# Two more token blocks of batch 0 by the seven-product form, with the work around them re-ordered, in an attention and squared-ReLU kernel

## The chip, the core and the metric

The kernel runs on one core of a Trainium2 chip. The metric is the device time of one execution in microseconds (us); the figure for the kernel before is the median of six runs. A core has a matrix engine (PE, its weight loads are listed as PEld), a vector engine (DVE), an activation engine (ACT), a general engine (POOL) and a sync engine (SP). Each of them works through its own instructions in order and waits on semaphores for the others. DMAs are issued by SP, ACT and POOL.

## What is computed

First a two-way cross attention between 512 tokens and 32 state rows for each of 8 batches and 8 heads of width 64, then a feed-forward layer on all 4352 rows:

```python
scores = scale * x @ state^T ; a = softmax(scores) ; xread = a @ state
scores2 = scale * state @ x^T ; a2 = softmax(scores2) ; sread = a2 @ x
X = concat([xread, sread], rows)      # (B*(512+32), 512)
h = X @ w_in                          # 512 -> 2048
r = maximum(h, 0)
g = s * (r * r) + b
out = g @ w_out                       # 2048 -> 512
```

`s` and `b` are single numbers, so they are applied after the last product: `out = s * ((r*r) @ w_out) + b * colsum(w_out)`. Inputs and outputs are float32; the products run in float16 with float32 accumulation.

## The kernel before

**Stages.** One loop runs over the batches s = 0 to 7, and within a batch over 16 feature blocks f of 128 columns of the hidden layer. For the token rows `xread @ w_in` is not formed as such: `state @ w_in` (tile M) is made once a batch, and `h` of block f is M times the softmax shares (`mm1_x`, two matmuls of 512 columns, a PSUM bank of pool psH with two buffers). `mm1_close` (L388) lets ACT take the ReLU into a tile r (three buffers, a pair of blocks each) and lets DVE square the pair into a tile g (L402). While the hidden layer of batch s is made, PE also does the output product of batch s-1, cut into single matmuls ("items") which are handed out between the blocks. Attention work of the next batch (M, T, E, D, V) is placed at given blocks by `pieces` (L782); "ahead" there means before the hidden block.

**The output product, plain.** For batch 0, `mm2_part` (L458) multiplies 16 blocks of g (weights 128x128) with 512 columns of w_out into one bank for each of the four token blocks of 128 rows: `units` (L680). `evac` (L442) scales, adds the bias and writes a tile `osb`, and POOL issues its DMA of 256 KB.

**The output product, seven products.** For batches 1 to 7, and for the 256 state rows ("sr"), `fast_items` (L506) computes the 2x2 block product of (two halves of the tokens) x (two halves of the hidden features) with (two halves of the features) x (two halves of the output columns) by seven block products P1 to P7 instead of eight. Each is 8 matmuls of 256 columns for each 128 tokens. It needs differences of w_out quarters (`weight_sums`, tiles wd0 to wd3, once) and sums of token halves of g (`token_sum`, tiles s1 to s4, eight DVE instructions a batch). Three PSUM banks are used, each by more than one product in turn, without being cleared:

- A: P1, read into qa (L585); then P2 is added to it, and the sum is written out (`put`, L559);
- B: P6, read into u2 (L588); then P7 is added, read into u3 (L593); then P4 is added and written out;
- C: P5 is written out with u3; then P3 is added and written out with u2.

So a product that is added to a bank can't start before DVE has read what the bank held. `put` writes a tile `osb` (pool opool, three buffers, shared with `evac`), which POOL sends out; a fourth tile waits until the DMA of the first has landed. The order of the products is the list in L626 to L632; for the last batch the tail has its own order and its own outputs (`put_last`, L569, DMA on SP).

**What sets the order.** PE, SP and POOL run in the order of the program text (L691). DVE and ACT are ordered by a scheduler, except where `tc.issue_after(...)` pins an instruction behind a named one; `G["last"]` names the latest square, `G["relu"]` the latest ReLU. POOL's queue holds the input loads (`load_x`) and nearly all outputs.

**Names used below.** "f = 9" is feature block 9 of batch 1 unless said otherwise. NST is the number of batches whose state is transposed by PE (`att_stT`); for the others one DMA transpose, `stT_dma`, issued by SP in batch 2, makes the tile stT_all. `mm1_sr` makes the hidden layer of the state rows (h_sr) at the end. The tail loop from L901 hands out the last batch's items with `go(rest, n)` after each h_sr block.

Of the kernel before, what the change touches and what calls it, by code (L numbers as in the profile page):

```python
# [14 lines left out]
def kernel(  # L15
# [10 lines left out]
    nc = tc.nc  # L26
# [15 lines left out]
    FC = 512  # L42
    NFC = DF // FC
    NPE = 2
    NST = 5
    NDT = 3
    NH = DM // 2
    TH = S // 2
# [339 lines left out]
    def mm1_close(key, hps, ntok, f):  # L388
        if f % 2 == 0:
            R2[key] = rpool.tile([P, 2, ntok], FP16, name=f"r_{key}_{f}", tag="r")  # L390
        r16 = R2[key]
        if key == 0 and f in (1, 5):
            nc.vector.tensor_scalar(r16[:, f % 2], hps, 0.0, None, ALU.max)
        else:
            nc.scalar.activation(r16[:, f % 2], hps, AF.Relu)  # L395
            G["relu"] = nc.cur_bb.bb.instructions[-1]
        if f % 4 == 0:
            G4[key, f // 4] = gpool.tile([P, 4, ntok], FP16, name=f"g_{key}_{f}", tag="g")
        gt = G4[key, f // 4]
        G[key, f] = gt[:, f % 4]  # L400
        if f % 2 == 1:
            nc.vector.tensor_mul(gt[:, f % 4 - 1 : f % 4 + 1], r16, r16)  # L402
            G["last"] = nc.cur_bb.bb.instructions[-1]

# [37 lines left out]
    def evac(ops, key, rr, n0, n1, dmas):  # L442
        osb = opool.tile([P, n1 - n0], FP32, name=f"osb_{key}_{rr}_{n0}", tag="osb")
        nc.vector.scalar_tensor_tensor(osb, ops, s_bc, bias_bc[:, n0:n1], ALU.mult, ALU.add)
        for eng, p0, p1, dst in dmas:
            eng.dma_start(dst, osb[p0:p1])

# [29 lines left out]
    def weight_sums():  # L477
        out = [[], []]
        for j in range(2):
            b11, b12 = wo[j][:, :, 0:NH], wo[j][:, :, NH:DM]  # L480
            b21, b22 = wo[2 + j][:, :, 0:NH], wo[2 + j][:, :, NH:DM]
            t1, t2, t3, t4 = (wd[i][j] for i in range(4))
            out[0] += [(t1, b12, b11), (t2, b22, t1)]
            out[1] += [(t3, b22, b12), (t4, b21, t2)]
        out = out[0] + out[1][::2] + out[1][1::2]
        return [lambda o=o, a=a, c=c: nc.vector.tensor_sub(o, a, c) for o, a, c in out]

    SQ = {}

    def token_sum(b, i, j):  # L490
        n = (B * Ns if b == "sr" else S) // 2
        SQ[b, i, j] = spool.tile([P, 4, n], FP16, name=f"s{i}_{b}_{j}", tag="s")
        o = SQ[b, i, j]
        a11, a21 = G4[b, j][:, :, 0:n], G4[b, j][:, :, n:]
        if i == 3:
            nc.vector.tensor_sub(o, a11, a21)  # L496
            return
        a12, a22 = G4[b, 2 + j][:, :, 0:n], G4[b, 2 + j][:, :, n:]
        if i == 1:
            nc.vector.tensor_add(o, a21, a22)  # L500
        elif i == 2:
            nc.vector.tensor_sub(o, SQ[b, 1, j], a11)  # L502
        else:
            nc.vector.tensor_sub(o, a12, SQ[b, 2, j])  # L504

    def fast_items(b):  # L506
        acc = {}
        kept = {}
        th = (B * Ns if b == "sr" else S) // 2
        ni = th // P  # L510

        def spare(name):
# [4 lines left out]

        def lhs(p, k, i):
            c = P * i
            if p == 1:  # L520
                return G[b, k][:, c : c + P]
            if p == 2:
                return G[b, 8 + k][:, c : c + P]
            if p == 4:
                return G[b, 8 + k][:, th + c : th + c + P]
            si = {3: 4, 5: 1, 6: 2, 7: 3}[p]
            return SQ[b, si, k // 4][:, k % 4, c : c + P]

# [10 lines left out]
        def keep(name):  # L539
            if b == "sr":  # L540
                i = len(kept)
                kept[name] = own[0][:, i : i + 1]
            else:
                kept[name] = upool.tile([P, 2, NH], FP32, name=f"{name}_{b}", tag=name)
            return kept[name]

        def put(bank, add, j, n0):
            if b == "sr":
                ends.append(own[1][:, len(ends) : len(ends) + 1])
                osb = ends[-1]  # L550
            else:
                osb = opool.tile([P, ni, NH], FP32, name=f"osb_{b}_{j}_{n0}", tag="osb")
            if bank == "C" and b == last_b:
                for i in range(ni):
                    nc.vector.scalar_tensor_tensor(
                        osb[:, i], acc["C", i], s_bc, add[:, i], ALU.mult, ALU.add
                    )
            else:
                nc.vector.scalar_tensor_tensor(osb, acc[bank], s_bc, add, ALU.mult, ALU.add)  # L559
            if b == "sr":  # L560
                for i in range(4):
                    dst = out_BSn[4 * j + i, S:ST, n0 : n0 + NH]
                    eng = nc.sync if i % 2 else nc.scalar
                    eng.dma_start(dst, osb[Ns * i : Ns * i + Ns, 0])
                return
            dst = out_BSn[b, 0:S].rearrange("(q ci cj) n -> cj q ci n", ci=2, cj=2)
            nc.gpsimd.dma_start(dst[j][:, :, n0 : n0 + NH], osb)  # L567

        def put_last(i):  # L569
            if not ends:  # L570
                ends.append(spare("osb_last"))
            osb = ends[0][:, i]
            nc.vector.scalar_tensor_tensor(
                osb, acc["C", i], s_bc, kept["u2"][:, i], ALU.mult, ALU.add
            )
            dst = out_BSn[b, 0:S].rearrange("(q ci cj) n -> cj ci q n", ci=2, cj=2)
            nc.sync.dma_start(dst[0][i][:, NH:DM], osb)

        def blk(n0):
            return bias_bc[:, n0 : n0 + NH].unsqueeze(1).broadcast_to([P, ni, NH])  # L580
# [42 lines left out]
            elif k == 7 and i == ni - 1:  # L623
                done(p)

        order = [(1, 0, 8), (6, 0, 4), (2, 0, 3), (6, 4, 8), (2, 3, 8), (7, 0, 8)]  # L626
        order += [(5, 0, 8), (4, 0, 8), (3, 0, 8)]
        if b == last_b:
            order = [(1, 0, 8), (6, 0, 4), (2, 0, 4), (6, 4, 8), (2, 4, 5)]
            order += [(7, 0, 8), (2, 5, 8), (4, 0, 8)]  # L630
        if b == "sr":
            order = [(p, 0, 8) for p in (1, 6, 2, 7, 5, 4, 3)]  # L632
        out = [(p, k, i) for p, k0, k1 in order for k in range(k0, k1) for i in range(ni)]
        if b == last_b:
# [43 lines left out]


    units = []  # L680
    for i in range(NKF):
        units.append((0, 2 * (i // 8) + i % 2, i % 8 // 2))
    last_b = B - 1

    def unit(u):
# [5 lines left out]
    with tc.manual_schedule(engines={ET.PE, ET.SP, ET.Pool}):  # L691
# [90 lines left out]
        def pieces(s):  # L782
# [6 lines left out]
            def ahead(f, fn):  # L789
                out.setdefault((f, "ahead"), []).append(fn)  # L790
# [44 lines left out]
            if s == 2:  # L835
                at(1, lambda: att_srT_dma(0))
                at(8, lambda: att_V(1))
                at(12, lambda: att_srT_dma(1))
            ahead(10, lambda: att_V(s))
            if nb < B:  # L840
                ahead(10, lambda: att_M(nb, 2, "later"))
                ahead(10, lambda: att_M(nb, 3, "later"))
                at(10, lambda: A[nb]["M", 2]())
                at(12, lambda: A[nb]["M", 3]())
            if s == last_b:
                at(11, lambda: att_srT(s))
            else:
                at(12, lambda: att_srT_dma(s))
            if s == last_b:
# [7 lines left out]
        for s in range(1, B):  # L857
# [3 lines left out]
            first = coming[s][:16] if s in fast else []  # L861
            if s == 1:
                items = [[] for _ in range(NKF)]
                for f in [*range(5), *range(6, 14)]:
                    items[f] = [lambda u=todo.pop(0): unit(u)]
                items[14], items[15] = first[0:8], first[8:16]
            else:
                flat = coming[s - 1][16:] + first
                n = -(-len(flat) // NKF)
                items = [flat[n * f : n * f + n] for f in range(NKF)]  # L870
            for f in range(NKF):
                for fn in todo_s.get((f, "ahead"), []):
                    fn()
                if s > 1 and 4 <= f < 13:
                    for fn in items[f]:
                        fn()
                    items[f] = []
                mm1_x(s, f)
                if s > 1 and f in (4, 5):
                    with tc.issue_after(G["last"]):  # L880
                        token_sum(s - 1, 4, f - 4)
                if s in fast:
                    if f in ((7, 9) if s == 1 else (7, 11)):
                        with tc.issue_after(G["last"]):
                            token_sum(s, 3, f // 8)
                    if s == 1 and f in (13, 14):
                        with tc.issue_after(G["last"]):
                            token_sum(s, f - 12, 0)
                    if s > 1 and f in (11, 12):
                        token_sum(s, f - 10, 0)  # L890
                    if f == 15:
                        token_sum(s, 1, 1)
                        token_sum(s, 2, 1)
                for fn in todo_s.get(f, []):
                    fn()
                if s == 1 and 5 <= f < 13:
                    with tc.issue_after(G["last"]):
                        sums.pop(0)()
                for fn in items[f]:
                    fn()  # L900
        rest = coming[last_b][16:]  # L901
# [6 lines left out]
        for f in range(4, NKF):  # L908
# [4 lines left out]
                token_sum("sr", 3, f // 8)  # L913
            if f in (11, 12, 13):
                token_sum("sr", (1, 2, 4)[f - 11], 0)
            go(rest, 5)
            if f >= 12:
                go(rows, 2)
        go(rest, 4)
# [37 lines left out]
```

## Time and profile before

| | us |
|---|---|
| median of six runs | 210.3 |
| lowest and highest run | 209.38 and 212.44 |
| the profiled execution, its own time | 209.38 |
| its span, first to last instruction | 207.6 |

| part of the profiled execution | us |
|---|---|
| last matmul ends | 202.9 |
| last DVE instruction (osb_last) starts | 202.94 |
| last output DMA is issued by SP | 203.6 |
| end of the span | 207.6 |

The page gives the busy time of each engine, the span in slices, the DMA queues, the chain of work that ended last, and groups of instructions. Two things to know in reading it: matmuls are pipelined, so the duration of one (380 ns for 512 columns, 273 for 256) includes its way through the array, and the pace is read from the distance of starts; and an engine's idle time matters only where the chain passes through it. The lowest DVE load of a 10 us stretch is at the start; between 20 and 30 us it is busy for 5.30 us, between 40 and 50 us for 8.59.

### The profile page before, as it was taken

Reading aid. Unit: us, or ns where it says so; the run is one execution under the profiler, and the core shown is the slowest. Engines: PE = TensorE matmul, PEld = TensorE weight load, DVE = VectorE, ACT = ScalarE, POOL = GpSimd, SP = SyncE. Lnnn points to the kernel's source line nnn. Section 1 sums busy time; section 2 is a strip of 40 time slices with the busy share of each in tenths; the row PEclk is TensorE's granted clock in tenths of the full one; section 3 lists DMA queues with packets and bytes.
Section 4 is the critical chain, followed back from the end, with each engine's and each line's share of the span. In section 5 each row is a group of like instructions: output and inputs, shape, how many; then the busy total and the mean of one; then the engine's idle time right before and its main releaser. Section 6 shows DMA issues by size and latency. Waiting matters only on the chain.

```text
span 207.6 us, 4792 instructions
## 1 busy us (share of the span) xinstructions
PE 199.1 (96%) x1949; PEld 130.1 (63%) x1949; DVE 159.9 (77%) x275; ACT 126.7 (61%) x252; POOL 37.6 (18%) x64
## 2 busy tenths in 40 slices
PE   7988999999999999999999999999999999999990
PEld 2433343445766776677667766666767776878880
DVE  1587835979769985999589968996799687696861
ACT  3678865699476857775776577666766455433100
POOL 5970001411210231023102110211021102100210
PEclk9999999999999999999999999999999999999999
DMA  6999996999998694949743904340425012100342
GB/s 184 225 202 206 206 192 100 184 175 172 242 103 178 152 159 71 176 114 207 103 95 88 201 26 104 84 124 3 101 74 137 0 54 101 55 0 0 103 123 83
DMA packets 46491, 25.49 MB, mean 123 GB/s; under 512 B 31428, under 2 KB 44484, under 8 KB 46468
## 3 DMA queue, kind: packets, MB, share of 16 engines
q0 software_dynamic: 15536, 16.19, 40.4%
q1 hardware_dynamic: 30132, 8.62, 23.2%
q10 hardware_dynamic: 800, 0.36, 0.7%
q8 instruction: 15, 0.25, 0.5%
q14 instruction: 8, 0.07, 0.1%
HBM read 17.33 MB, written 8.91 MB: 126 GB/s over the span
## 4 chain that ended last, share of the span: by engine, by line
PE 90%; DVE 4%; ACT 3%; issue 0%
PE h L70 25%; PE oB L70 18%; PE oC L70 12%; PE oA L70 12%; PE o L70 7%; PE Mps L70 4%; PE warm_ps L70 3%; PE h_sr L70 2%; ACT r L395 2%; PE V L70 1%; PE oB_sr L70 1%; PE T L70 1%; DVE M L320 1%; PE oC_sr L70 1%; PE oA_sr L70 1%; DVE g L402 1%
## 5 line engine op out<-in xcount | busy, mean ns | idle before, releaser
L395 ACT ACTIVATE r<-h 128x512 f16<-128x512 f32 x126 | 74.4, 602 | 46.7 <-PE h L70 46.6
L70 PE MATMUL h<-a,M 128*128 128x512 f16 x256 | 74.3, 380 | 1.2 <-DVE M L320 0.6
L402 DVE TENSOR_TENSOR g<-r 128x1024 f16<-128x1024 f16 x64 | 43.5, 682 | 16.0 <-ACT r L395 15.4
L70 PEld LDWEIGHTS <-s 128*128 128x128 f16 x448 | 43.3, 98 | 17.1 <-DVE s L502 1.7
L70 PEld LDWEIGHTS <-g 128*128 128x128 f16 x400 | 37.7, 98 | 20.6 <-issue 5.2
L567 POOL DMA_DIRECT2D out_dram<-osb x27 | 18.2, 675 | 124.5 <-DVE osb L559 85.4
L70 PE MATMUL oB<-wd,s 128*128 128x256 f16 x224 | 32.6, 273 | 0.2 <-DVE u L588 0.2
L70 PEld LDWEIGHTS <-M 128*128 128x128 f16 x256 | 24.5, 98 | 12.9 <-issue 1.8
L70 PE MATMUL oA<-wo,g 128*128 128x256 f16 x224 | 31.7, 273 | 0.1
L297 ACT CAST M<-Mps 128x1024 f16<-128x1024 f32 x20 | 20.1, 1007 | 0.0
L70 PE MATMUL oC<-wd,s 128*128 128x256 f16 x112 | 16.5, 273 | 0.0
L70 PE MATMUL o<-wo,g 128*128 128x512 f16 x64 | 16.3, 381 | 0.0
L70 PE MATMUL oB<-wd,g 128*128 128x256 f16 x112 | 15.9, 273 | 0.0
L70 PE MATMUL oC<-wo,s 128*128 128x256 f16 x112 | 15.3, 273 | 0.0
L395 ACT ACTIVATE r_sr<-h_sr 128x256 f16<-128x256 f32 x16 | 6.1, 382 | 8.7 <-PE h_sr L70 8.7
L588 DVE SCALAR_TENSOR_TENSOR u<-oB,s_bc,qa 128x512 f32<-128x512 f32 x7 | 5.3, 751 | 6.1 <-PE oB L70 6.1
L234 ACT ACTIVATE E<-T 128x256 f16<-128x256 f32 x20 | 7.4, 384 | 4.0 <-PE T L70 4.0
L502 DVE TENSOR_TENSOR s<-s,g 128x1024 f16<-128x1024 f16 x14 | 9.6, 684 | 0.2
L70 PE MATMUL h_sr<-srdT,wi 128*128 128x256 f16 x64 | 9.6, 273 | 0.0
L504 DVE TENSOR_TENSOR s<-g,s 128x1024 f16<-128x1024 f16 x14 | 9.6, 684 | 0.0
L496 DVE TENSOR_TENSOR s<-g 128x1024 f16<-128x1024 f16 x14 | 9.6, 684 | 0.0
L500 DVE TENSOR_TENSOR s<-g,g 128x1024 f16<-128x1024 f16 x14 | 9.5, 682 | 0.0
(107 smaller groups left out, 206.0 us busy)
## 6 DMA issues: line engine op xcount, KB each, us to landing
out_dram<-osb POOLq DMA_DIRECT2D x31, 256.0 KB, 3.7
xn<-in_x_dram POOLq DMA_DIRECT2D x7, 512.0 KB, 8.7
wi<-in_moe_w_in_dram POOLq DMA_DIRECT2D x4, 512.0 KB, 9.0
wo<-in_moe_w_out_dram POOLq DMA_DIRECT2D x4, 512.0 KB, 15.9
xf<-in_x_dram SPq DMA_DIRECT2D x2, 512.0 KB, 4.8
out_dram<-osb_sr SPq DMA_DIRECT2D x8, 32.0 KB, 1.5
out_dram<-osb_sr ACTq DMA_DIRECT2D x8, 32.0 KB, 1.7
out_dram<-osb_last SPq DMA_DIRECT2D x2, 128.0 KB, 2.3
```

Source lines behind the costliest of these rows:

```text
L70: return nc.tensor.matmul(out, lhsT, rhs, start=start, stop=stop, tile_position=tp, is_transpose=is_transpose, skip_group_check=True,)
L234: nc.scalar.activation(a["E"][:, g, 256 * m : 256 * m + 256], Ts[m][:, g, :], AF.Exp, scale=scale, accum_out=a["rs"][:, NG * m + g : NG * ...
L297: nc.scalar.copy(dst, ps)
L320: nc.vector.tensor_copy(dst[:, 0], two[0])
L395: nc.scalar.activation(r16[:, f % 2], hps, AF.Relu)
L402: nc.vector.tensor_mul(gt[:, f % 4 - 1 : f % 4 + 1], r16, r16)
L496: nc.vector.tensor_sub(o, a11, a21)
L500: nc.vector.tensor_add(o, a21, a22)
L502: nc.vector.tensor_sub(o, SQ[b, 1, j], a11)
L504: nc.vector.tensor_sub(o, a12, SQ[b, 2, j])
L567: nc.gpsimd.dma_start(dst[j][:, :, n0 : n0 + NH], osb)
L588: nc.vector.scalar_tensor_tensor(u, acc["B"], s_bc, kept["qa"], ALU.mult, ALU.add)
```

## The change

- Token blocks 0 and 1 of batch 0 stay in the plain form. Blocks 2 and 3 become a small seven-product form, "0b", whose two token halves are these two blocks of 128 rows. Its 56 items are handed out seven at a time at f = 6 to 13 of batch 1, in place of eight parts of four matmuls. Its four outputs of 128 KB go through `osb` and POOL.
- It needs two sums of tokens at f = 0, two at f = 1, one each at f = 7 and 8, two at f = 10; the weight differences move from f = 5 to 12 to f = 0, 1, 2 and 6 to 9, and their order within the list changes. Token sums of batch 1 move from f = 7, 9 to f = 10, 12.
- The squares of the pairs that end at f = 5 and 9 of batch 1 are done by ACT.
- `evac` sets `G["last"]`.
- NST falls from 5 to 4: batch 4's state is transposed by the DMA.
- The product order of batches 1 to 6 keeps P2 in two parts of four and four; the last batch's P2 is split 3, 3, 2 around P6 and P7.
- In batch 7 the items follow the hidden block at f = 4 to 12 too; V is made at f = 4 and srT at f = 6; the tail's counts of items change.
- The last output tile's first half goes out on ACT's queue, its second in two halves of 64 rows on SP's and ACT's queues.

```diff
-    NST = 5
+    NST = 4
...
-        if f % 2 == 1:
+        if key == 1 and f in (5, 9):
+            with tc.issue_after(nc.cur_bb.bb.instructions[-1]):
+                nc.scalar.square(gt[:, f % 4 - 1 : f % 4 + 1], r16)
+        elif f % 2 == 1:
             nc.vector.tensor_mul(gt[:, f % 4 - 1 : f % 4 + 1], r16, r16)
             G["last"] = nc.cur_bb.bb.instructions[-1]
...
         nc.vector.scalar_tensor_tensor(osb, ops, s_bc, bias_bc[:, n0:n1], ALU.mult, ALU.add)
+        G["last"] = nc.cur_bb.bb.instructions[-1]
...
-        out = out[0] + out[1][::2] + out[1][1::2]
+        out = out[0][::2] + out[0][1::2] + out[1][::2] + out[1][1::2]
...
+    def span_of(b):
+        if b == "sr":
+            return "sr", 0, B * Ns // 2
+        return (0, TH, P) if b == "0b" else (b, 0, TH)
...
+            if b == "0b":
+                nc.gpsimd.dma_start(x_dst(0, 2 + j)[:, n0 : n0 + NH], osb[:, 0])
+                return
...
-            nc.sync.dma_start(dst[0][i][:, NH:DM], osb)
+            if i == 0:
+                nc.scalar.dma_start(dst[0][i][:, NH:DM], osb)
+                return
+            for eng, p in ((nc.sync, 0), (nc.scalar, P // 2)):
+                eng.dma_start(dst[0][i][p : p + P // 2, NH:DM], osb[p : p + P // 2])
...
-        order = [(1, 0, 8), (6, 0, 4), (2, 0, 3), (6, 4, 8), (2, 3, 8), (7, 0, 8)]
+        order = [(1, 0, 8), (6, 0, 4), (2, 0, 4), (6, 4, 8), (2, 4, 8), (7, 0, 8)]
...
-            order = [(1, 0, 8), (6, 0, 4), (2, 0, 4), (6, 4, 8), (2, 4, 5)]
-            order += [(7, 0, 8), (2, 5, 8), (4, 0, 8)]
-        if b == "sr":
+            order = [(1, 0, 8), (6, 0, 4), (2, 0, 3), (6, 4, 8), (2, 3, 6)]
+            order += [(7, 0, 8), (2, 6, 8), (4, 0, 8)]
+        if ni == 1:
             order = [(p, 0, 8) for p in (1, 6, 2, 7, 5, 4, 3)]
...
-    for i in range(NKF):
-        units.append((0, 2 * (i // 8) + i % 2, i % 8 // 2))
+    for i in range(8):
+        units.append((0, i % 2, i // 2))
...
-            ahead(10, lambda: att_V(s))
+            ahead(4 if s == last_b else 10, lambda: att_V(s))
...
-                at(11, lambda: att_srT(s))
+                at(6, lambda: att_srT(s))
...
-                for f in [*range(5), *range(6, 14)]:
+                half = fast_items("0b")
+                for f in range(5):
                     items[f] = [lambda u=todo.pop(0): unit(u)]
+                for f in range(6, 14):
+                    items[f] = [half.pop(0) for _ in range(7)]
...
-                if s > 1 and 4 <= f < 13:
+                if 1 < s < last_b and 4 <= f < 13:
...
-                    if f in ((7, 9) if s == 1 else (7, 11)):
+                    if f in ((10, 12) if s == 1 else (7, 11)):
                         with tc.issue_after(G["last"]):
-                            token_sum(s, 3, f // 8)
+                            token_sum(s, 3, int(f > 10))
...
-                if s == 1 and 5 <= f < 13:
+                if s == 1:
                     with tc.issue_after(G["last"]):
-                        sums.pop(0)()
+                        for _ in range({0: 2, 1: 1, 2: 1, 6: 1, 7: 1, 8: 1, 9: 1}.get(f, 0)):
+                            sums.pop(0)()
+                        for i, j in {0: [(1, 0), (2, 0)], 1: [(1, 1), (2, 1)], 7: [(3, 0)], 8: [(3, 1)],
+                                     10: [(4, 0), (4, 1)]}.get(f, []):
+                            token_sum("0b", i, j)
...
-            go(rest, 5)
+            go(rest, (4, 3, 5, 5, 5, 5, 5, 5, 5, 6, 6, 6)[f - 4])
```

`span_of` gives `token_sum` and `fast_items` the key of g, the first token and the number of tokens in a half; "0b" reads columns 256 to 511 of batch 0's g.

More of the change, by code (lines that the diff above doesn't have):

```diff
@@ L484, in weight_sums @@
             out[1] += [(t3, b22, b12), (t4, b21, t2)]
-        out = out[0] + out[1][::2] + out[1][1::2]
+        out = out[0][::2] + out[0][1::2] + out[1][::2] + out[1][1::2]
         return [lambda o=o, a=a, c=c: nc.vector.tensor_sub(o, a, c) for o, a, c in out]
     SQ = {}
+    def span_of(b):
+        if b == "sr":
+            return "sr", 0, B * Ns // 2
+        return (0, TH, P) if b == "0b" else (b, 0, TH)
     def token_sum(b, i, j):
-        n = (B * Ns if b == "sr" else S) // 2
+        key, c0, n = span_of(b)
         SQ[b, i, j] = spool.tile([P, 4, n], FP16, name=f"s{i}_{b}_{j}", tag="s")
         o = SQ[b, i, j]
-        a11, a21 = G4[b, j][:, :, 0:n], G4[b, j][:, :, n:]
+        a11, a21 = G4[key, j][:, :, c0 : c0 + n], G4[key, j][:, :, c0 + n : c0 + 2 * n]
         if i == 3:
@@ L497, in token_sum @@
             return
-        a12, a22 = G4[b, 2 + j][:, :, 0:n], G4[b, 2 + j][:, :, n:]
+        t2 = G4[key, 2 + j]
+        a12, a22 = t2[:, :, c0 : c0 + n], t2[:, :, c0 + n : c0 + 2 * n]
         if i == 1:
@@ L508, in fast_items @@
         kept = {}
-        th = (B * Ns if b == "sr" else S) // 2
+        key, c0, th = span_of(b)
         ni = th // P
@@ L519, in lhs @@
             c = P * i
+            a = c0 + c
             if p == 1:
-                return G[b, k][:, c : c + P]
+                return G[key, k][:, a : a + P]
             if p == 2:
-                return G[b, 8 + k][:, c : c + P]
+                return G[key, 8 + k][:, a : a + P]
             if p == 4:
-                return G[b, 8 + k][:, th + c : th + c + P]
+                return G[key, 8 + k][:, th + a : th + a + P]
             si = {3: 4, 5: 1, 6: 2, 7: 3}[p]
@@ L543, in keep @@
             else:
-                kept[name] = upool.tile([P, 2, NH], FP32, name=f"{name}_{b}", tag=name)
+                kept[name] = upool.tile([P, ni, NH], FP32, name=f"{name}_{b}", tag=name)
             return kept[name]
```

## The prediction

> **What bounds the kernel now.** I read the page's busy rows first, then the chain of waits, then single stretches of the timeline.
>
> ```profile
> PE 199.1 (96%) x1949; PEld 130.1 (63%) x1949; DVE 159.9 (77%) x275; ACT 126.7 (61%) x252; POOL 37.6 (18%) x64
> PEclk9999999999999999999999999999999999999999
> PE 90%; DVE 4%; ACT 3%; issue 0%
> ```
> TensorE at full clock makes nine tenths of the chain. A busy PE may still be a slow one, so I look at its pace. In the chain of waits between 36 and 54 us (start, length, what):
>
> ```profile
> 37.25 0.86 PE o L70 x4
> 38.54 0.86 PE o L70 x4
> 46.34 0.43 PE D L70 x2
> 50.16 0.87 PE oA L70 x8
> 52.88 0.76 PE oB L70 x7
> ```
> Four matmuls of 512 columns take 0.86, so one is 0.216 us; eight of 256 take 0.87, so one is 0.109. Columns per time are equal and the matmuls follow without a hole, here and up to 173 us. After that the chain leaves PE several times:
>
> ```profile
> 174.63 0.61 ACT r L395
> 181.43 0.67 DVE qa L585
> 185.40 0.76 DVE u L588
> 190.40 0.33 PE oA L70 x3
> ```
> The timeline's PE starts give the size of the holes there (distance of two starts less the streaming time): h of batch 7, block 13, waits 0.41 at 175.28; oA waits 0.23 for qa at 182.15; oB waits 0.35 for u at 186.20; oB waits 0.17 at 190.73. Together 1.16 us.
>
> Third, how fast an output block leaves. All output of batch 0 goes through three osb buffers. Asked for that tile between 39.9 and 41 us, and for POOL's timeline, the trace says:
>
> ```profile
> 39.15 0.87 POOL L120 DMA_DIRECT2D xn<-in_x_dram  x1
> 40.01 1.13 POOL L446 DMA_DIRECT2D out_dram<-osb  x2
> ```
> ```profile
> L446 POOL DMA_DIRECT2D out_dram<-osb x2: 562/570/577, 40.0 to 40.6; - x2
> DMA to landing us min/median/max: 7.7/7.7/7.7
> ```
> The first two output blocks are issued at 40.0 and 40.6, behind a 512 KB input load, and land 7.7 us later, at 47.7 and 48.3. Nobody waits for that now: the fourth osb is written at 50.83.
>
> **The change part by part.**
>
> 1. *Token blocks 2 and 3 of batch 0 by seven products.* 32 matmuls of 512 columns go (32 x 0.216 = 6.9), 56 of 256 come (56 x 0.109 = 6.1): -0.86 us of PE, or 0.108 at each of steps f = 6 to 13 of batch 1 (seven small ones, 0.76, for four large ones, 0.86). The Trainium skill, "TensorE: Matmul & The Clock Gate", section "Back-to-back issue gap", speaks against it: it gives 131 ns per matmul at 512 columns and 81 at 128 for streams of weight load and matmul. With some 98 between them (my estimate from these two) the sum would be 56 x 0.098 - 32 x 0.131 = +1.3 us. The chain above shows 216 and 109, so I take -0.86.
>
> 2. *What the seven products ask of VectorE.* Added: eight token sums of 128x512 (0.34 from start to start by the chain's g_sr row) and seven scalar_tensor_tensor of 128x256 plus one add (0.40); removed: two evacuations of 128x512 (0.66) and two squares (0.60). About 8 x 0.34 + 8 x 0.40 - 1.3 - 1.2 = +3.4 us of DVE between 27 and 52 us. It fits in total (DVE idles 4.7 us of 20-30), and the early pieces hide: differences and sums at f = 0 and 1 end near 32, where DVE now waits until 32.75 for wsum. But the new products have deadlines, because each bank is accumulated again after it is read:
>  - Product 7 may not start before u2 has read bank B. DVE in the new order from 37.56: stT 0.20, difference 0.60, bias_d 0.33, qa 0.40; then the square of r6 waits for relu 7, which now stands behind ScalarE's new square (37.73 + about 0.97, as R's step; so relu 7 ends at 39.3); then square, difference, sum, difference, sum: 39.32 + 0.60 + 0.60 + 0.34 + 0.60 + 0.34 = 41.80, and u2 ends at 42.28. PE gets there at f = 9 at 41.65: a hole of 0.68.
>  - Product 3 may not start before the put of product 5 has read bank C. That put writes the fourth osb tile since the start, so it takes the first one's buffer and must wait until the first block has landed: 47.7. It ends at 47.76 + 0.48 = 48.24. PE reaches product 3 (last item of f = 12) at 46.6 without any hole, at 47.3 after the one before. The put decides, product 7's hole vanishes inside it: PE resumes at 48.29, 1.68 us late.
>  Step 13 then starts at 48.40 instead of 47.48. Queued behind the waiting put on DVE are the square of block 10, a token sum, the put of product 4, a_2 and the square of block 12; by the same steps the put of product 4 ends at 49.84 (first oA of batch 1 at 50.8) and a_2 at 50.4 (wanted at 53), so no second hole. The balance of 1 and 2: -0.86 + 1.68 = +0.82.
>
> 3. *Two squares of batch 1 on ScalarE.* Two of about 1.05 us (row R, 128x1024, 1058 ns). ACT is full from 43 to 51 us; with both, relu 13 ends near 49.7 and relu 14 near 51.5, and they are wanted at 51.7 and 53.0 once PE is 0.8 late. Zero, hidden under part 2; without that hole h_0 of batch 2 would wait about 0.4.
>
> 4. *Batch 4's state transpose by the DMA* (NST): two PE transposes less (stTps x2, 0.11 in the chain's kind of row), -0.11. The stT_all transpose is issued at 70.3 and lands 4.2 later; grown from six to eight blocks it lands near 76 (4.2 x 8/6) and is wanted near 78. SP's later srdT transposes move about 0.4, wanted at the very end. Zero.
>
> 5. *Queues.* On POOL batch 4's load now stands behind two outputs, 41.1 to about 49; it has until 62 (its transpose's issue). SP keeps its order.
>
> 6. *The last batch's order.* Items now follow the hidden block instead of preceding it, so h13 has 1.19 us of other PE work between it and h12 and needs 0.86: the 0.41 goes. P2 starts after 3.35 us of work behind h15 where qa needs 3.21: the 0.23 goes. Six P2 items, not two, stand between P6 and P7 (1.5 us against 1.0): the 0.35 goes. Four oA, two oA_sr and h_sr14 lie between P7 and P4: 1.08 against 1.01, the 0.17 goes. Sum -1.16; next late would be P4, with 0.07 to spare. V and srT, moved earlier, cost the same and wait for nothing new.
>
> 7. *The last output in two halves on two queues.* The trace has 2.8 us for the last 128 KB, 1.9 for the one before, 1.5 to 1.9 for 32 KB: between 0 and -1.1. The Trainium skill, "DMA: Bandwidth & Descriptors", "Issuing engines are not separate DMA queues", says that other issuing engines save only issue time; by it the gain is about 0.2, by the 1.9 row it is 0.9. I take -0.3, nearer the rule: the 2.8 us row holds the same bytes on the same engines.
>
> Sum: 0.82 - 0.11 - 1.16 - 0.3 = -0.75. The profiled execution (209.38, span 207.6) is 0.9 below the median of 210.3; the difference is applied to the median: 209.5.
>
> **Rivals.**
>  - *The put's wait doesn't bite.* The first block could land a microsecond and a half earlier, as the neighbouring 3.7 us median of output DMAs would allow. Then u2's 0.68 remains: -0.86 + 0.68 - 0.11 - 1.16 - 0.3 = -1.75; if VectorE is quicker than I laid out, -2.4. 207.9 to 208.5. For it: the landing depends on what else the DMA engines carry. Against: the 512 KB ahead of it are the same in both kernels.
>  - *Slower: batch 4's load meets batch 3's transposes.* The xT transpose issued at 46.3 takes 8.6 us to land (54.9), and T of batch 3 reads it at 57.4 (58.2 after part 2). The load moved to 49 would share the engines with it. If the whole 7.0 us of the load ahead of it (39.15) were added, it would land at 61.9, a hole of 3.7: +2.9, 213.2. It decides above +0.75, so beyond a landing at 59. Against: in the kernel before the same load runs ahead of the transpose and delays it already.
>  - *The end's reordering only moves its holes:* -0.75 + 1.16 = +0.4, 210.7.
>
> **Chances.** Forecast 0.58 (209.5, own range 208.3 to 210.6), first rival 0.30, slower rival 0.05, the last 0.07. One per cent (2.1 us) is about what a measurement of this kernel tells from no change, the six runs spanning 209.4 to 212.4. Faster by more: most of the first rival and a little of the forecast's edge, 0.32; slower by more: 0.05; the rest 0.63. Range 207.6 to 210.8: the first rival's middle, the forecast with the tail's bounds, the last rival.
>
> **What would show it.** For: PE's product 3 of batch 0 waiting over a microsecond near 47-48 us on DVE's put, and that put on an output DMA; no PE hole above 0.1 between 173 and 191; the stT copy of batch 4 gone. Against: PE without a hole at f = 12, or u2 named as the wait; T of batch 3 waiting for xT; last landing still 2.8 us.

## The result, and the profile after

| | before | after |
|---|---|---|
| median, us | 210.29 (67 runs, 209.38 to 212.98) | 209.44 (30 runs, 208.4 to 212.51) |
| ratio | | 0.996, 95% interval 0.9947 to 0.9973 |
| profiled execution: own time, span | 209.38, 207.6 | 208.74, 207.0 |

The kernel gains 0.85 us, between 0.57 and 1.11. 209.5 was forecast. The terms behind it came out otherwise, as the rest shows. A ratio leaves out executions more than 1.5% above the fastest of their kernel, and the profiles of e6, e12 and e13 below are of such executions (15 of the 22 of e6, 2 of the 10 of e12, 1 of the 8 of e13).

PE still carries the chain that ended last, but no longer as alone as before. Part 4 of the page of after (shares by engine, then by line):

```profile
PE 85%; DMA 5%; DVE 4%; ACT 3%; issue 1%; POOL 1%; ACTq 0%
PE h L70 24%; PE oB L70 18%; PE oC L70 11%; PE oA L70 11%; PE Mps L70 4%; PE o L70 3%; PE h_sr L70 3%; DMA stf<-in_state_dram 2%; DMA a<-aT 2%; ACT r L395 2%; PE V L70 1%; PE oB_sr L70 1%; PE T L70 1%; PE oB_0b L70 1%; DVE M L320 1%
```

The 2% of DMA a<-aT are new. The 2% of the state load lie in the first 10 us: the first product of batch 1 comes 0.5 us later in this execution than in that of before. Most profiles below differ so: batch 1 starts between 26.98 us (e1) and 28.51 us (e8), and in e3, which has the head of before unchanged, 0.9 us later than in before. No part of the change explains it. The profile of before is of the fastest of its 67 runs (209.38).

Three stretches answer to the prediction. A hole is given as in the prediction, as the distance of two starts less the streaming time; the bracket of a timeline line counts from the end of the matmul before and is smaller. First, the head of batch 1 in after, from the timeline (start, length, engine, operation; in brackets the idle time ahead of it and its releaser):

```profile
42.25 0.48 DVE L608 SCALAR_TENSOR_TENSOR u_0b<-oB_0b,s_bc,qa_0b 128x256 f32<-128x256 f32 x1
...
42.78 0.60 PE L70 MATMUL oB_0b<-wd,s_0b 128*128 128x256 f16 x4 [0.48 <-DVE u_0b L608]
...
47.03 0.48 DVE L572 SCALAR_TENSOR_TENSOR osb_0b<-oC_0b,s_bc,u_0b 128x256 f32<-128x256 f32 x1
...
47.79 0.27 PE L70 MATMUL oC_0b<-wo,s_0b 128*128 128x256 f16 x1
...
50.09 0.48 DVE L572 SCALAR_TENSOR_TENSOR osb_0b<-oB_0b,s_bc,qb_0b 128x256 f32<-128x256 f32 x1 [1.38 <-PE oC_0b L70]
...
50.63 0.60 PE L70 MATMUL oA<-wo,g 128*128 128x256 f16 x4
```
```profile
DMA to landing us min/median/max: 6.8/8.1/9.3
```

Product 7 waits for u2 as laid out: from start to start the step is 0.65 us longer than a matmul of 256 columns. The put of product 5 (47.03) does not hold up product 3 (47.79, behind six matmuls without a pause). The put of product 4 does hold up oA of batch 1: the step ahead of 50.63 is 0.31 us longer than the matmul. The second fence is the row of landings of the first two output blocks. Issued at 40.10 and 40.67, they landed at 46.91 and 49.97. The timeline calls the releaser of 50.09 "PE oC_0b". But the second landing is 0.12 us ahead of it, in e2 below the same put runs at 49.29 with those matmuls going on until 50.48, and in e4, where it takes no earlier buffer, the wait is gone: it is the wait for the block whose buffer it takes. A release by a landing can be printed under another name.

Second, the end. Three stretches of after, and the second and third of before (length, then busy us and instructions of PE, PEld, DVE, ACT and POOL, then clock, DMA share, GB/s):

```profile
164.00:174.00 10.00, 10.00 (x107) 7.29 (x105) 7.77 (x14) 5.19 (x11) 1.35 (x2) 1.00 0.12 44
174.00:182.00 8.00, 8.00 (x68) 6.39 (x67) 6.45 (x12) 4.04 (x10) 1.35 (x2) 1.00 0.23 81
182.00:192.00 10.00, 10.00 (x94) 8.97 (x92) 8.25 (x18) 3.83 (x10) 0.00 (x0) 1.00 0.00 0
```
```profile
174.00:182.00 8.00, 7.75 (x63) 5.96 (x61) 6.38 (x11) 4.08 (x10) 0.91 (x2) 1.00 0.20 69
182.00:192.00 10.00, 9.75 (x87) 8.35 (x86) 7.76 (x18) 3.44 (x10) 0.00 (x0) 1.00 0.00 0
```

PE is busy without a pause in after, which it was not in before. The holes of 0.41, 0.23, 0.35 and 0.17 are gone and none above 0.1 has come.

Third, a hole that the prediction has no word on. The chain of after near 117 us (start, length, what):

```profile
112.42 4.61 DMA a<-aT
117.03 0.05 issue
117.07 0.61 PE h L70 x2
```

The transpose of aT for batch 5 landed after 4.6 us where it took 3.4 in before, and PE stood 0.27 us.

### The profile page after: what moved, and what is told of

Same layout as the page of the kernel before. It is cut to its first block, busy times and chain, and to the rows that moved or that the text cites. A ratio compares the mean times of both kernels' runs of the same rounds, so it can differ in the third digit from the quotient of the medians.

```text
span 207.0 us, 4853 instructions
## 1 busy us (share of the span) xinstructions
PE 197.4 (95%) x1971; PEld 132.2 (64%) x1971; DVE 163.4 (79%) x286; ACT 128.4 (62%) x254; POOL 39.0 (19%) x66
## 4 chain that ended last, share of the span: by engine, by line
PE 85%; DMA 5%; DVE 4%; ACT 3%; issue 1%; POOL 1%; ACTq 0%
PE h L70 24%; PE oB L70 18%; PE oC L70 11%; PE oA L70 11%; PE Mps L70 4%; PE o L70 3%; PE h_sr L70 3%; DMA stf<-in_state_dram 2%; DMA a<-aT 2%; ACT r L395 2%; PE V L70 1%; PE oB_sr L70 1%; PE T L70 1%; PE oB_0b L70 1%; DVE M L320 1%
## 5 line engine op out<-in xcount | busy, mean ns | idle before, releaser
L405 DVE TENSOR_TENSOR g<-r 128x1024 f16<-128x1024 f16 x62 | 42.2, 682 | 12.2 <-ACT r L395 11.4
L70 PEld LDWEIGHTS <-g 128*128 128x128 f16 x392 | 37.2, 98 | 18.8 <-issue 4.8
L70 PE MATMUL oA<-wo,g 128*128 128x256 f16 x224 | 32.5, 273 | 0.1
L572 DVE SCALAR_TENSOR_TENSOR osb<-oC,s_bc,u 128x512 f32<-128x512 f32 x12 | 8.9, 744 | 0.4 <-PE oC L70 0.4
```

Of the source, the lines that this page charges most:

```text
L70: return nc.tensor.matmul(out, lhsT, rhs, start=start, stop=stop, tile_position=tp, is_transpose=is_transpose, skip_group_check=True,)
```

## The experiments

Ratios are to the kernel before on the same chip. Where a saving in us is given, it is (1 - ratio) x 210.4. "Parts 1 to 3" are the seven products with their sums, differences and squares, the "new end" is part 6 (the last batch's order), the "split" is part 7 (the last output in pieces on two queues).

| run | what it is | ratio | interval |
|---|---|---|---|
| e1 | before + new end | 0.9921 | 0.9897 to 0.9944 |
| e2 | before + parts 1 to 3 | 0.9988 | 0.9969 to 1.0008 |
| e3 | before + split | 1.0006 | 0.9989 to 1.0024 |
| e4 | after + outputs of 0b in own space | 0.9945 | 0.992 to 0.997 |
| e7 | after again | 0.996 | 0.9941 to 0.998 |
| e8 | after without parts 1 to 3 | 0.9984 | 0.9966 to 1.0002 |
| e5 | e4 + u2 early | 0.9943 | 0.992 to 0.9966 |
| e6 | e5 + two outputs on SP | 1.0004 | 0.9975 to 1.0032 |
| e9 | e1 + NST = 4 | 0.9949 | 0.9929 to 0.9969 |
| e11 | before + parts 1 to 3 + new end | 0.9932 | 0.9914 to 0.995 |
| e12 | e11 + own space + u2 early | 0.9898 | 0.9867 to 0.9929 |
| e13 | e12, squares on VectorE | 0.9919 | 0.989 to 0.9948 |

**e1, the new end alone.** The change in the last batch's order, on the kernel before:

```
-            order = [(1, 0, 8), (6, 0, 4), (2, 0, 4), (6, 4, 8), (2, 4, 5)]
-            order += [(7, 0, 8), (2, 5, 8), (4, 0, 8)]
+            order = [(1, 0, 8), (6, 0, 4), (2, 0, 3), (6, 4, 8), (2, 3, 6)]
+            order += [(7, 0, 8), (2, 6, 8), (4, 0, 8)]
...
+            ahead(4 if s == last_b else 10, lambda: att_V(s))
...
+                at(6, lambda: att_srT(s))
...
+                if 1 < s < last_b and 4 <= f < 13:
...
+            go(rest, (4, 3, 5, 5, 5, 5, 5, 5, 5, 6, 6, 6)[f - 4])
```

> The kernel before with the last batch's new order alone: V and srT earlier, items behind the hidden block, six P2 items before P7, the counts per step. My sum (step 6): -1.16 us, no PE hole above 0.1 us between 173 and 191 us, so a ratio near 0.9945. The rival that the order only moves its holes: 0, ratio 1.000, with new holes in the same stretch.

Measured 0.9921, that is -1.7 us (-1.2 to -2.2). PE in e1:

```profile
174.00:182.00 8.00, 8.00 (x70) 6.58 (x69) 6.45 (x12) 4.08 (x11) 1.23 (x2) 1.00 0.20 69
182.00:192.00 10.00, 10.00 (x94) 8.96 (x92) 7.79 (x17) 3.70 (x10) 0.17 (x1) 1.00 0.00 0
```

The holes are gone and the time with them: the rival that they only move is out. The same edit on e2 (e11 against e2, 0.9932 against 0.9988) is worth 1.2 us, the sum's own figure.

**e2 and e8, parts 1 to 3 alone, and all but them.** e2 takes back in after the end, the split and NST; e8 takes back the 0b products, the moved weight differences and token sums and the squares. The new order of P2 in batches 1 to 6 goes with parts 1 to 3 in both; it was not run alone.

> The changed kernel without the new end, the split of the last output and NST = 4: so the seven products for token blocks 2 and 3 of batch 0, the weight differences and the two squares on ScalarE alone. My sum (steps 1 to 3): +0.82 us, ratio 1.004. As I read the trace of the changed kernel, where the waits at P7 and at the last bank came to 0.65 + 0.31 us instead of 1.68: -0.86 + 0.95 = +0.1, with the later wait for batch 5's aT +0.3 at most, ratio 1.000 to 1.002. The rival without the put's wait: -0.2, ratio 0.999.

> The changed kernel without parts 1 to 3 (token blocks 2 and 3 of batch 0 as in the kernel before): so the new end, the split and NST = 4. By e1 and e3: -1.2 to -1.7 us, ratio 0.992 to 0.9945. If parts 1 to 3 cost 0.8 us as my sum had it, e7 is 0.8 us slower than this kernel; if they are even, as e2 says (-0.25 with an interval from -0.65 to +0.17), the two are the same. No hole near 117 us here, since in e1 and in the kernel before aT lands in 3.4 us.

e2: -0.25 us (-0.65 to +0.17). e11 against e1, which differ by the same parts, gives +0.2; e7 against e8 -0.5. The forecast +0.8 is refuted by e2; the parts are about even. In the profile of e2 product 7 waits 0.64, the last bank 0.08 and aT of batch 5 0.50. The put of product 5, which was to hold PE for a microsecond, and the product behind it in e2:

```profile
47.68 0.48 DVE L572 SCALAR_TENSOR_TENSOR osb_0b<-oC_0b,s_bc,u_0b 128x256 f32<-128x256 f32 x1 [0.42 <-PE D L70]
...
48.22 0.27 PE L70 MATMUL oC_0b<-wo,s_0b 128*128 128x256 f16 x1
```

The first block landed at 47.56, 0.12 us ahead of this put, as above. So the put did wait for it, and PE, which came to product 3 only at 48.14, lost 0.08.

**e3, the split of the last output alone.**

```
-            nc.sync.dma_start(dst[0][i][:, NH:DM], osb)
+            if i == 0:
+                nc.scalar.dma_start(dst[0][i][:, NH:DM], osb)
+                return
+            for eng, p in ((nc.sync, 0), (nc.scalar, P // 2)):
+                eng.dma_start(dst[0][i][p : p + P // 2, NH:DM], osb[p : p + P // 2])
```

> The kernel before with only the split of the last output over two queues. My sum (step 7): -0.3 us, and a gap from the last DVE instruction to the last landing of about 2.7 us. The page's rule: -0.2. The single profiles of before and after differ by 0.41 us in that gap: ratio 0.998. If the 1.9 us row held: -0.9, ratio 0.996.

Measured +0.1 us (-0.2 to +0.5): nothing. The gap from the last DVE instruction to the last landing in seven profiles of whole outputs is 3.02 (before), 2.96 (e1), 2.49, 2.41, 2.42, 2.50 and 2.36 us, mean 2.6; in six with the split 2.61 (after), 3.11 (e3), 2.61, 2.63, 2.66 and 2.60, mean 2.7. The 3.02 of before was a high draw from one spread. The last landings of after and, in the second fence, of e11 (whole), both as the least, median and greatest of the last batch's own output:

```profile
L597 SPq DMA_DIRECT2D out_dram<-osb_last x1: 553/553/553, 203.2 to 203.2; - x1
L597 ACTq DMA_DIRECT2D out_dram<-osb_last x1: 580/580/580, 203.2 to 203.2; - x1
...
DMA to landing us min/median/max: 1.9/2.3/2.6
```
```profile
DMA to landing us min/median/max: 1.9/2.0/2.2
```

Half the bytes on ScalarE's queue land after 2.6 us; the whole on SP's lands after 2.2. The issues are quicker with two queues (0.03 us from the last DVE instruction, not 0.19), and that is all.

**e7, the changed kernel again.**

> The changed kernel once more, beside e8, which differs from it by parts 1 to 3 alone: ratio to the kernel before 0.996 as in the first result. If the wait of h of batch 5 for aT belongs to the kernel and not to one execution, PE has again a hole of 0.2 us or more near 117 us.

0.996 again. The profile has the hole of batch 5, now 0.99 us:

```profile
117.77 0.61 PE L70 MATMUL h<-a,M 128*128 128x512 f16 x2 [0.83 <-DMA a<-aT]
```

So it belongs to the kernel. Every profile with parts 1 to 3 has it (after 0.27, e2 0.50, e4 0.93, e5 0.14, e7 0.99, e11 1.19, mean of these six 0.67; e6, e12 and e13 0.62, 0.14 and 0.62), and of the five without them none has (before, e1, e3, e8, e9). e7 has no wait at the put of product 4, nor has e2; the 0.31 of the first profile is not in every execution.

**e4, outputs of 0b in space of their own.** The four results go to the second halves of the kept sums' tiles, which hold nothing.

```
-                kept[name] = upool.tile([P, ni, NH], FP32, name=f"{name}_{b}", tag=name)
+                t = upool.tile([P, 2, NH], FP32, name=f"{name}_{b}", tag=name)
+                kept[name] = t[:, 0:ni]
+                if b == "0b":
+                    spares.append(t[:, 1:2])
...
+            elif b == "0b":
+                osb = spares.pop(0)
```

> The changed kernel, with the four outputs of token blocks 2 and 3 of batch 0 written to space of their own (the unused second halves of the kept sums), so that no put waits until an earlier output block has landed. Trace of the changed kernel: the wait at the put of P5 did not hold PE, the one at the put of P4 held it 0.31 us; so the gain over the changed kernel is 0.3 us (ratio to the kernel before 0.9945), and the P7 hole of 0.65 stays. My forecast's sizing: 1.0 us gained (1.68 - 0.68), ratio 0.991. If the 1.38 us wait before that put was for PE and not for a landing: no gain, and the wait stays.

0.9945, 0.3 us under e7, with intervals that overlap, so that a gain is not shown. The wait at 50 is gone, but e7 had none either; the one at 42 is 0.64. A full microsecond was not there to be had. The profile also has a small case of the slower rival: xT of batch 3 lands at 58.64 (54.09 in after), and T waits for it (0.43 us by the bracket).

**e5, u2 early.**

```
-                        for _ in range({0: 2, 1: 1, 2: 1, 6: 1, 7: 1, 8: 1, 9: 1}.get(f, 0)):
+                        for _ in range({0: 2, 1: 1, 2: 1, 3: 1, 6: 1, 10: 2}.get(f, 0)):
...
+                if b == "0b":
+                    G["last"] = nc.cur_bb.bb.instructions[-1]
```

> e4 with the weight differences for product 7 made at steps 3 and 6 and those for product 4 put behind u2, so that u2 ends about 1.2 us earlier than 42.7. By the trace product 7 then does not wait: no hole at 42, 0.65 us less than e4, ratio to the kernel before 0.991. If the hole had only covered another that comes later (put of P5 or P4), the same time as e4, 0.9945.

0.9943, no gain over e4, though the hole at 42 is gone. From the timeline of e5:

```profile
41.41 0.48 DVE L614 SCALAR_TENSOR_TENSOR u_0b<-oB_0b,s_bc,qa_0b 128x256 f32<-128x256 f32 x1
...
46.86 0.22 ACT L243 ACTIVATION_READ_ACCUMULATOR E<-T 128x1 f32 x1
...
47.13 0.38 PE L70 MATMUL D<-E,bones 128*128 128x512 f16 x1 [0.20 <-ACT E L243]
```

u2 starts 0.84 us earlier than in after (and in an execution 0.36 later at its head). But PE now comes to D of batch 2 before its exponentials: two steps there are 0.13 and 0.36 us too long. Of the 0.65, 0.49 is a new wait, for ScalarE, and 0.16 is left. The second theory, that the hole had covered another, was right, but the other wait is for ScalarE and not for a put.

**e6, two of the outputs on SP.**

```
-                nc.gpsimd.dma_start(x_dst(0, 2 + j)[:, n0 : n0 + NH], osb[:, 0])
+                eng = nc.sync if not spares or len(spares) == 2 else nc.gpsimd
+                eng.dma_start(x_dst(0, 2 + j)[:, n0 : n0 + NH], osb[:, 0])
```

> e5 with two of the four outputs of token blocks 2 and 3 issued by SP, so that POOL issues as many DMAs as in the kernel before. In the traces one POOL issue of each kernel, always at the same place in POOL's own order, leaves 0.95 us behind its put and not 0.29; the two more issues of the change moved it from the second output of batch 4 to the first, and aT of batch 5 then landed in 4.6 to 4.8 us and not in 3.4. Theory: here the late issue is the second output again, aT lands in 3.4 us, and the hole near 117 us (0.27 to 0.93) is gone: 0.3 to 0.9 us less than e5, ratio 0.987 to 0.990. If the slow landing has another cause, the hole stays and the time is that of e5.

The ratio is 1.0004, 1.3 us above e5 with intervals that do not meet, and the median of all 22 executions is 213.06: the theory fails. The profiled execution (214.3) shows another wait. From the timeline of e6, POOL and PE, and two stretches:

```profile
39.82 0.88 POOL L120 DMA_DIRECT2D xn<-in_x_dram  x1
...
44.01 0.91 POOL L120 DMA_DIRECT2D xn<-in_x_dram  x1
...
61.91 0.65 PE L70 MATMUL T<-xT,stT 64*32 64x256 f16 x16 [4.06 <-DMA xT<-xn]
```
```profile
60.00:64.00 4.00, 2.04 (x28) 0.95 (x29) 0.55 (x1) 1.35 (x7) 0.00 (x0) 0.71 0.76 150
64.00:68.00 4.00, 3.75 (x25) 2.59 (x25) 2.66 (x7) 2.23 (x6) 0.68 (x1) 0.86 0.67 126
```

T waits 4.06 us for xT of batch 3, which lands only at 61.87, and the granted clock is 0.71 and 0.86 in the stretches around and after it. This is the wait that the slower rival named, a landing beyond 59 with a hole near 3.7, here with batch 4's load issued earlier instead of later: at 44.0, an output less ahead of it, where after has 48.3. The load of batch 3 then lands at 49.4 (45.9 in after). That the earlier load is the cause is argued, not shown: in before batch 4's load left earlier still, at 41.1, and batch 3's landed at 46.1; in e4 it left at 48.5, and batch 3's landed as late as 48.3.

POOL's late issue did fall on the second output of batch 4 again, as the theory wanted, yet aT of batch 5 landed only after 4.96 us and PE waited 0.62 for it. That speaks against the theory, as far as one execution can.

**e9 and e11, where -1.7 went.** e1 alone is better than the changed kernel, so something in it costs.

> e1 with batch 4's state transpose by the DMA as well (NST = 4), without the split. e1 came to 0.9921 and e8, which adds NST = 4 and the split to it, to 0.9984: 1.3 us between them, where I had -0.1 for NST and -0.3 for the split, and the split alone (e3) measured +0.1. If NST = 4 is what costs: the time of e8, 0.998. If NST is worth its two transposes, as my step 4 had it: 0.9915 to 0.992, and the split is at fault only together with the new end.

> The changed kernel with NST = 5 and an undivided last output: parts 1 to 3 and the new end. By e1 (-1.66) and e2 (-0.25), added: -1.9 us, ratio 0.991. If NST = 4 and the split cost nothing here: the time of the changed kernel, 0.996.

e9: 0.9949, 0.6 us more than e1. e8 adds the split to that and has 0.9984. e11, which leaves out both, has 0.9932, 0.6 us less than e7. Neighbouring intervals touch, those of e1 and e8 do not: NST = 4 and the split together take 0.6 to 1.3 us back, where the sum had -0.4. How it divides between them is not shown; the new end with the split but without NST = 4 was not run. Part of it can be seen: in e8 and e9 aT of batch 4, 20 us after the larger state transpose, lands after 5.17 and 4.63 us, and PE stands 0.83 and 0.29. From the chain of e9:

```profile
90.97 4.63 DMA a<-aT
95.59 0.05 issue
95.64 0.60 PE h L70 x2
```

SP's own issue of this transpose is longer there. In e9 and, in the second fence, in after:

```profile
90.97 1.94 SPq L290 DMA_TRANSPOSE a<-aT  x1
```
```profile
91.32 1.23 SPq L290 DMA_TRANSPOSE a<-aT  x1
```

It takes 1.94 us in e9 and 2.04 in e8, and 1.23 or 1.24 in each of the other twelve profiles, so 0.7 to 0.8 us of the late landing is issue. No other profile has this wait, after and e4, e5, e7 with NST = 4 included, so how it hangs together with NST = 4 stays open, and so does the split's part. e9 has two more holes that before, e1 and e8 do not have, 0.38 at 111.5 for a put and 0.24 at 120.3; e3, without NST = 4, has the same two (0.42 and 0.25), so they do not come from it.

**e12, the parts that pay, together.** e11 with the edits of e4 and e5, and

```
-        nc.gpsimd.memset(ones16, 1.0)
-        nc.gpsimd.memset(mean16, 1.0 / Ns)
+        nc.vector.memset(ones16, 1.0)
+        nc.vector.memset(mean16, 1.0 / Ns)
```

> e11 with the sums of e5 (u2 early), outputs of token blocks 2 and 3 in space of their own, and two memsets of the start on VectorE, so that POOL's late issue falls on the second output of batch 4 again. No hole at 42 (0.65) and none at 50 (0.31); aT of batch 5 lands in 3.4 us if it is the distance to that output that counts (0.9 us in the changed kernel, 1.5 before), else in 4.5 to 5 and PE waits near 117. By e4 and e5: 0.3 us less than e11; with the holes' whole size 1 us less.

0.9898: 2.1 us under the kernel before, about 1.3 under the changed one and 0.7 under e11. It is the lowest ratio of all, though its interval overlaps those of e1 and e11. The memsets did nothing: POOL's late issue stays on the first output, and aT landed after 4.5 us, with a hole of 0.14. There is a price. Three of its ten executions took 210.3 to 212.7 us. From the profiled one, VectorE and PE:

```profile
69.40 1.22 DVE L278 TENSOR_REDUCE den<-ET 128x32 f32<-128x1024 f16 x1 [3.14 <-DMA ET<-E]
70.53 0.74 DVE L578 SCALAR_TENSOR_TENSOR osb<-oC,s_bc,u 128x512 f32<-128x512 f32 x1
...
71.33 0.60 PE L70 MATMUL oC<-wo,s 128*128 128x256 f16 x4 [2.20 <-DVE osb L578]
```

PE stood 2.2 us for a put. That put takes the fourth `osb` tile of this kernel, and the first had landed at 48.1, so its buffer was free. It stood behind `den` on VectorE, which had waited 3.14 us for the transpose ET of batch 3, issued at 60.27. Landings were slow all through this stretch: ET of batch 2 took 14 us, an output issued at 60.52 took 8.8. The profile of e13 has the same wait (3.99 us for ET, PE's hole 2.95 at 71.48).

**e13, the squares back on VectorE.**

```
-        if key == 1 and f in (5, 9):
+        if key == 1 and f in ():
```

> e12 with both squares of batch 1 on VectorE again (part 3 undone). My step 3 had the two squares on ScalarE at zero. But in e5 and e12, with u2 early, PE waits 0.49 us near 46.5 for E of batch 2, and ScalarE is busy without a pause from the copy of M at 41 until then, with one of the squares (1.06 us) in between. Theory: without it E comes about a microsecond earlier and the wait of 0.49 is gone: 0.5 us less than e12, ratio 0.987 to 0.988. Rival: the 1.2 us more on VectorE hold up u2 or a put, with a hole of 0.3 to 0.6 near 42 or 48 to 50 instead: the time of e12 (0.990). Squares at zero also here: no change of the 0.49 us wait.

0.9919, 0.4 us more than e12, with intervals that overlap. The ratio does not show the theory's gain, and the trace shows the rival. From its timeline:

```profile
45.55 0.47 DVE L617 SCALAR_TENSOR_TENSOR u_0b<-oB_0b,s_bc,qa_0b 128x256 f32<-128x256 f32 x1
...
46.08 0.38 PE L70 MATMUL oB_0b<-wd,g 128*128 128x256 f16 x2 [1.14 <-DVE u_0b L617]
46.30 0.59 PE L70 MATMUL h<-a,M 128*128 128x512 f16 x2
46.73 0.59 PE L70 MATMUL D<-E,bones 128*128 128x512 f16 x2
```

D no longer waits for ScalarE, as the theory said, but product 4 now waits for u3 on VectorE, a hole of 1.31 us (1.14 by the bracket), where the rival had 0.3 to 0.6. At this place neither of the two engines takes the squares without a wait.

## Why the prediction was right, point by point

By its own list of signs the main forecast failed, though its number held: PE did not wait over a microsecond at product 3, and u2 was named as the wait. That is the first rival's picture, whose sum, -1.75, was not measured either.

- *Step 1, seven products: -0.86.* The 56 small matmuls of after start 0.109 us after one another in the median, as taken. Of 312 matmuls with 512 columns none is followed in less than 0.214, so the 131 ns of the Trainium skill ("TensorE: Matmul & The Clock Gate", "Back-to-back issue gap"), which would have made the step a loss, is not reached here. By the prediction's own figures the gain is 32 x 0.216 - 56 x 0.109 = 0.81, not 0.86.
- *Step 2, waits of +1.68.* This is the mis-sized term. The load on VectorE was right: 159.9 us busy before, 163.4 after, +3.5 for the +3.4 laid out. So was the hole at product 7: 0.68 forecast, 0.65 measured in after, 0.64 in e2 and e7. The put's hold on PE was not. In e2 and e7 the put of product 5 waited for the landing and ended at 48.17 and 48.16, close to the 48.24 forecast. But PE came to product 3 at 48.14 and 48.17, not at 47.3, since batch 1 had started 0.83 and 0.86 us later in these executions than in that of before, while the landing had not moved: PE lost 0.08 and 0.04. In after batch 1 started 0.48 later, the block landed at 46.91 instead of 47.7, and the put held nothing. So the wait was the distance between two clocks, PE's and the transfers', both read from one execution of before. The put of product 4, given as free, held 0.31 in after and at most 0.03 in e2, e7 and e11. In all 0.65 to 0.95 in place of 1.68: the rival in which the put doesn't bite was nearer here than the forecast.
- *Step 3, squares at zero.* Nothing speaks against it in the changed kernel, but the squares were never undone there. They stand under the wait at product 7; once that is closed (e5), ScalarE holds PE for 0.49 us. In e13, with that wait closed, undoing them moves the hole to VectorE and the ratio says 0.4 us more, within the noise.
- *Step 4, NST -0.11, and step 7, split -0.3.* Neither gain is measured. The split alone is nothing (e3): the rule that other issuing engines save issue time only (the Trainium skill, "DMA: Bandwidth & Descriptors", "Issuing engines are not separate DMA queues") fits what the runs show, 0.16 us of issue, and the 2.8 us row of before was a single draw from 2.2 to 2.8. With the new end the two together cost 0.6 to 1.3 us, for reasons only partly seen.
- *Step 5, queues at zero.* Right for what it named: xT of batch 3 landed at 54.8 in before and 54.1 in after. It missed aT of batch 5, which had 0.64 us to spare in before and which no step counted: 0.14 to 1.19 us of wait.
- *Step 6, the end: -1.16.* Right: holes gone, -1.2 us between e2 and e11, -1.7 in e1 with an interval down to -1.2.

That the total, -0.75 against -0.85, came out right is luck. By the runs, parts 1 to 3 were 1.1 us better than their +0.82 (e2: -0.25), the new end 0.5 better than its -1.16 in e1 (about as forecast between e2 and e11), and NST = 4 with the split 1.0 to 1.7 us worse than their -0.4. These errors happen to cancel. The holes do not account for all of it: with 0.81 gained and 0.65, 0.31 and 0.27 lost in after, parts 1 to 3 should cost 0.4 us, and e2 measured at most +0.17. That rest stays open; the new order of P2 in batches 1 to 6, to which the prediction gave no figure, is among what could have made it.

## What to carry to other kernels

A wait on a landing that the trace of before shows once is a draw from a spread (6.8 and 9.3 us for two like blocks, 0.6 us apart in their issue, here): write it as a range, and ask of every transfer with under a microsecond to spare who else will be on the engines then. A hole that is closed is worth what the next wait leaves of it (0.16 of 0.65 in e5), so look up the next one before counting. The order on a shared queue is part of the design: two of its outputs moved to another queue (e6) made the kernel 1.3 us slower than e5 by the ratio, and 15 of its 22 executions took 212.4 us or more. And a sum that comes out right shows little before its terms have been run apart.

## What the hardware showed that I had not expected

- In all fourteen profiles one POOL issue past 110 us leaves 0.94 to 0.97 us behind its put, where its neighbours leave 0.29 to 0.31 behind theirs. In the kernels without the 0b outputs it is the second output of batch 4; with them on POOL the first; in e6, with two of the four on SP, the second again; two memsets less (e12) change nothing. The change puts two more issues ahead of it on POOL, which together carry 256 rows more, as many as one output of batch 4, and the late issue moved forward by one output. That fits a count of rows and not one of instructions. What holds it the traces don't show.
- Where the late issue is the first output, that output leaves 1.03 us ahead of aT of batch 5 and not 1.70, the next one follows aT by 0.91 us and not 1.54, and aT lands after 4.5 to 5.5 us and not 3.3 to 3.45. The output behind aT can't be the whole cause: behind aT of batches 3 and 7 an output follows after 0.88 in after too, and these land after 3.1. The output ahead is left as a suspect, but in e6, with the spacing of before (1.70 and 1.54), aT landed after 4.96. The cause stays open.
- After PE stood still for some microseconds its clock was halved for a while: in e12, after 2.2 us of waiting at 71, matmuls of 512 columns came every 0.426 us near 74 and not every 0.216. In the stretch below the granted clock is 0.57. The profiles of e6 and e13 show the same after their long waits (clock 0.71 and 0.57). There a long wait cost more than its length.

```profile
72.00:76.00 4.00, 4.00 (x18) 2.26 (x17) 3.67 (x6) 2.18 (x4) 0.92 (x2) 0.57 0.58 144
```
